# A third batch's u goes through the DMA transpose, the pair units' last product is cut in two, and the written order of all groups is drawn anew

## The chip, the core and the metric

The kernel runs on one core of a Trainium2 chip. Its engines are TensorE (PE, with its weight loads as PEld), VectorE (DVE), ScalarE (ACT), GpSimd (POOL) and SyncE (SP, which only issues transfers); each runs its own instructions in the order in which they were written. The metric is device time in microseconds (us). Times stand beside a profile, which is one execution recorded by the hardware.

## What is computed

Four batches of 768 steps with 8 heads of 48 columns (384 columns in all). First a gated linear recurrence, then a mixer that works along the steps with rank 32 and along the columns with a hidden width of 1536:

```python
for t in range(S):                                    # S = 768, per batch and head
    state = alpha[:, :, t, :, None] * state + einsum('bhd,bhe->bhde', k[:, :, t], v[:, :, t])
    y[:, :, t] = einsum('bhd,bhde->bhe', q[:, :, t], state)
x = y.transpose(0, 2, 1, 3).reshape(B, S, H * D)      # [4, 768, 384]
h = x.transpose(0, 2, 1) @ U @ V                      # U [768, 32], V [32, 768]
u = x + h.transpose(0, 2, 1)
out = u + relu(u @ w_ch1) @ w_ch2                     # w_ch1 [384, 1536], w_ch2 [1536, 384]
```

All inputs and the output are float32; the kernel multiplies in bfloat16.

## The kernel before

**Chunks.** Each batch b has six chunks c of 128 steps. Of a chunk, alpha, k, q and v are loaded as tiles of 128 steps x 8 heads x 48 columns, 192 KB each. All six chunks of batch 0 and the first four of batch 1 are worked as "pair units": two chunks are loaded together by halves of the heads, so that two neighbouring steps of a head lie in one run of 384 bytes (`pload`, line 350). The chunks of batches 2 and 3 and the last two of batch 1 are plain: one step of one head is a run of 192 bytes (`load`, line 357). The names below are those of the groups in the program, with b.c or b.half behind.

**A chunk's recurrence.** ACT takes the logarithm of alpha (lines 380 and 551), PE sums it along the steps, ACT takes exponentials, k and q are scaled by them (`rk`, lines 411 and 579, on POOL or DVE) and transposed on PE (`tr`, lines 428 and 592) or, for batch 3, by a DMA transpose that SP issues (`tkq`, line 604). Scores are masked (`pm`), multiplied with v (`rv`, cast by ACT or POOL), the state is carried on (`st`), and the result is copied out as x. In a pair unit the last product is `py`: 16 small matmuls (line 535) that need two masked tiles, one for the even heads and one for the odd.

**The mixer.** Per batch: the product with U (`xu`, line 702) and its copy (`utx`, line 713), the product with V chunk by chunk (`hb`, line 716), the sum u on DVE (line 717), and then u transposed, two chunks at a time. For the batches in `QUEUE_U` this is one DMA transpose on SP per two chunks (`tu`, line 722); for the others six PE transposes (`utr`, line 736) and a copy of the PSUM bank on ACT or DVE (`uev`, lines 277 and 279). `mlp1` (line 765) is 24 groups a batch, twelve for each half of the steps, of three matmuls each. The first half needs the transposes of chunks 0 to 3, the second those of chunks 2 to 5:

```python
if b in QUEUE_U:
    need = [(uT, "c", c) for c in ((0, 1), (1, 2))[tt]]
else:
    need = [(uT, 0), (uT, 1)] if tt == 0 else [(uT, 1), (uT, 2)]
```

A `relu` on ACT (line 775) or DVE (line 777) follows each; `mlp2` (line 791) is three groups of four matmuls for each chunk, then DVE adds u (line 797) and SP stores (lines 800 and 802).

**What sets the order.** Nothing is scheduled when the kernel is built. Every group is added to a plan, and the strings `TABLE` and `SLOTS` say in which order the groups are written, on which engine, and which buffer each takes. Three characters of `TABLE` are one group: two for its number and one for the engine (P for PE, A for ACT, D for DVE, G for POOL, S for SP; for a transfer the letter is the engine that issues it). "++" is a string of filler matmuls (line 270) that compute nothing. A group that needs another engine's result waits for it, and all that is written behind it on its own engine waits with it. Transfers are counted on eight semaphores in turn, so an engine that issues a transfer first waits for the one eight before it.

Of the kernel before, what the change touches and what calls it, by code (L numbers as in the profile page):

```python
# [16 lines left out]
ArA++BAASAvSA-AA3SQPAAySAsSCLA++BCNPAtSAzA++BA5ACOACPAAwS++BCiADSAECAAxSBAACRGAuS++BCSGCjACQACkPA4SClA++BCmAA7ADUPDVADWA  # L17
A0SC5ACTPCoGCUPCWABDSDXAEEPEGAA6SCpDA9ACVDCxPC7P++BCnACMAC9AAFGC+ABBSDrAA2SCyDCqPCsDCaPBHSCbDCXPCzPEFAA8SCrPCYDDtPCtAA1S
CcPCZDCeP++BCdDC8ADYGDaPCuPDZDCfPEIGDcAC-GDTGCwDEKPEHAAJPDbPC0DBCABFSABSDhPGCAAKADwA++BChACvDDiPDdDDjDEJGDvADuAA+SDePDgD
AGPELPAHADkPEMDC1PDfDBEAENABGSC2PBLSC3DDyGD0PD2ABISCgDBJSBKSBPSGEPDlDC6GGGADIPDJPDKDEOPDxGDLPDAGGHAEDGDBPC4DDzPDnPERPEPD  # L20
GFAAMSDMDALGDCPDDADmPDoPEQDESPD1AAQSDEABMSGJGDpAD3PGZAETDD5DDFPEUPDGDGIGDqAGbPDNPEVPGDGDOPD6P++BDsAGcADHDEWPEXAD4DD7PD8D
DPPDRAEYDGKPGMAD9PAYSGLPGNDACGADPD+PD-PEADGRPGSDDQAAEAEBAGOPGPDEZPEaPBTSGfGGwAGeAGdAEbAGyPG1ABNSGTD++BG0AEqPGQDBRSEoPGhP
GVPErDEkPGgGGWPGzABQAEcPEiPGjAEpDElDGiPGaGEsPHJAAUSAOGGXAEePEjDEtAAPGGkDGYAEdDHLPBOSHMAHNAEfDEmPGlPEnDANGGoPEgPGpDFGPGmD
GqDFHDFIPATABVSGnDFKPARGEhAFLAEwPExAASGFMPFNAE4PE2PAaGFQPE5DEyPBXSG2GBUSAZAFRDAbAFAPFJAE0PAcSE3ABSABZSFEPFFAGrDHOAG4PG6A
G3DHPDE1DFBAEuPHRPHTDFOPHQGEzDFPDG5PHiAFcPAXAFaPEvDG7AFdAAVAHSPHUDGsPGtPGuDBYSGvAG8PG+DAWGAhSBWSGxGGUGBaSAmSHVPBfSBrSG-P
FbAHkPHmAHoAFWPHADHBGE6PHXDH4AHnAFSPHlAG9DHqGFYPFTDH6PE7DH7AH8AHWDE+PHsPHuDHCDHpGE8PHKAFXAFZAHrPHtDFUPFVABbSE-AE9DHEPAgA
HFPHGPHYPHZDAfGBtSBjSHHDHvPHdPHIDHwDH+GIAPFCPAeGHaGAdAH9GHePFePHbDAiABcSHcDHxDICDFDAFkPF2PH-PIBDF8PIDPAlAHfPAjGAkGF9PBeS
HgAFwPBhSIFDHDGIEDHjABnSHyPH2PH3AH5AHzDH0DF3PFlPH1DIGPHhAApAFfPIHAIIPFxPIJAIQPISPAoGIKPAnGIRDITDAqGF+PFyPILDIMPINDFgPIYP
IZDF-DFzDF4PKCAKEPLBABkSIWPKFABzSJuAIXDIUPIOPIVAIPDKXAFmPFnDIaPBqSIbDJwPJxAF5DJ1DIiPKZPJvAIjAKdAI0PBlSFhDKGABdSAIGJyAJEP
JFABvSB1SIgPKKGJ2GI1AI+PI-AKIAIyPI4PKsAI5AIzAJGPIhDBiSI6PI7AJ0AJzAImPIqPKHAIrAInAKaAJKPIwPKDGJ+PJHAIkPKbAKuPKwAJIPLDPJLD  # L30
KcAKMPJ-DLWABwSJAPJJAIuPKyAJBAKfGIlDKeDKvAIxDBgSKJGLGAI2PI3DLHAIvAIcPLEABsSLIGIdAIePIfAKgPKiDJ3PBpSB0SIoPBmSJ5DLFAIpANFA
KxAIsPKhPItAJ4PKODKjAKSPKTDKLPJSPJTPJ6DBoSK0GJ7PLJGKNAB6SBySKUGKtGJ9DKkPKlDKPPKRDJUPLYPLZANHPKmDNJANKAKYGFqPFrPNNGKzGLKP
I8PNLAJ8DNIAKQDKnPBxSLaALcGKqPLMALLPLbDKoDKpGLNAB-SFsPK2PLdPK4DI9AKVPFtDK8PLfABuSK9DKrAJCPJDAK1PK3DLePNMGLgACDSK+GKAPKWA
JkPB3SB2SKBDB7SJVDB5SNWALOPNOSLPDK5PK6DLhPOMAJlPLQDK7DLCGLRPLSDLTGJmPNYPOOPCISORALXAN6ACESNbANoANcAJePLjDLUPLiDNaAK-PLAD
LVDJpPLkPJfPLlANZANPPNeGLmPLnAN8PN9ANGGN-ANQDJqPB4SLvPLtPN+ANRDOAANdGJrPCHSLwDOQALqPCCSLuDCASLxSLrDNXAOeALoPJYPLpDJMPNSP
# [821 lines left out]
```

## Time and profile before

| | |
|---|---|
| time, three runs | 158.62 us median (157.86 to 159.13) |
| span of the profiled execution | 156.8 us, 1.8 under the median |
| PE busy | 148.8 us, 95% of the span |
| DVE, ACT, POOL busy | 107.6, 90.0, 61.4 us |
| DMA | 31.53 MB, mean 201 GB/s |
| chain of waits | PE 84%, DMA 8%, DVE 4% |
| issued from ACT's queue (q10) | 2.16 MB of the 31.53 |

A page of the profile gives the busy time of each engine, then the span in 40 slices (tenths busy, the granted clock of PE, DMA share and GB/s), the chain that ended last, and groups of instructions by line. The granted clock of PE is 1.00 in every stretch shown. In a window row the pairs are busy time and, in brackets, the instructions of PE, PEld, DVE, ACT and POOL, and the last three numbers are the clock, the DMA share and GB/s. The DMA share counts the time that packets are in work on the 16 DMA engines, and can pass 1 where packets of two queues overlap.

### The profile page before, as it was taken

How to read it: one execution, taken by the hardware profiler on the slowest of the kernel's cores; microseconds unless marked ns; L12 is line 12 of the kernel's file. 1: busy time of each engine (PE TensorE's matmuls, PEld its weight loads, DVE VectorE, ACT ScalarE, POOL GpSimd, SP SyncE). 2: the span in 40 equal slices, each digit the busy share in tenths (PEclk: the TensorE clock that was granted, in tenths of full speed). 3: DMA queues.
4: the chain of work that ended last, by engine and by line, in shares of the span. 5: the costliest groups of instructions: out<-in, count | busy, mean ns of one | idle time of the engine just before them, and what ended most of it. 6: DMA issues, size and time to landing. Idle time of an engine off the chain costs nothing.

```text
span 156.8 us, 4413 instructions
## 1 busy us (share of the span) xinstructions
PE 148.8 (95%) x1715; PEld 97.7 (62%) x1715; DVE 107.6 (69%) x236; ACT 90.0 (57%) x234; POOL 61.4 (39%) x95
## 2 busy tenths in 40 slices
PE   2878999999999999999999999999999999999992
PEld 0456678666767656666668666665667555556662
DVE  6038899987899628816588976885989580673162
ACT  3678889986978272999958585379232202450000
POOL 8285995756088600136679261052623000000000
PEclk9999999999999999999999999999999999999999
DMA  5999999999988989989989996897976346345625
GB/s 145 319 323 326 268 301 313 344 265 268 280 239 193 270 161 191 189 169 211 208 169 214 134 222 119 169 181 145 176 144 151 105 87 139 127 129 151 199 100 201
DMA packets 98291, 31.53 MB, mean 201 GB/s; under 512 B 91968, under 2 KB 98240, under 8 KB 98272
## 3 DMA queue, kind: packets, MB, share of 16 engines
q1 hardware_dynamic: 92464, 29.11, 80.6%
q10 hardware_dynamic: 5808, 2.16, 5.2%
q8 instruction: 13, 0.21, 0.6%
q14 instruction: 6, 0.05, 0.1%
HBM read 23.79 MB, written 4.72 MB: 182 GB/s over the span
## 4 chain that ended last, share of the span: by engine, by line
PE 84%; DMA 8%; DVE 4%; ACT 1%; issue 1%; ACTq 0%; DVEq 0%
PE ps L791 30%; PE ps L765 29%; DMA io<-in_alpha_dram 8%; PE ps L716 3%; PE ps L620 3%; PE ps L592 2%; PE ps L687 2%; PE ps L428 2%; PE ps L535 2%; PE ps L558 2%; PE ps L682 1%; PE ps L736 1%; PE ps L452 1%; PE ps L643 1%; PE ps L702 1%; DVE rkq L411 1%
## 5 line engine op out<-in xcount | busy, mean ns | idle before, releaser
L791 PE MATMUL ps<-w_sb,h1t 128*128 128x384 bf16 (+2 forms) x300 | 53.1, 319 | 0.0
L765 PE MATMUL ps<-uT,w_sb 128*128 128x384 bf16 x288 | 51.0, 326 | 0.1
L775 ACT ACTIVATE h1t<-ps 128x384 bf16<-128x384 f32 x58 | 27.2, 509 | 19.1 <-PE ps L765 19.0
L791 PEld LDWEIGHTS <-h1t 128*128 128x128 bf16 x300 | 27.3, 97 | 15.9 <-issue 0.6
L765 PEld LDWEIGHTS <-w_sb 128*128 128x128 bf16 x288 | 27.0, 98 | 16.3 <-issue 0.4
L777 DVE TENSOR_SCALAR h1t<-ps 128x384 bf16<-128x384 f32 x38 | 20.1, 552 | 19.4 <-PE ps L765 15.9
L579 POOL TENSOR_TENSOR rkq<-io,aa 128x384 bf16<-128x384 f32 x12 | 11.7, 975 | 23.0 <-ACT aa L569 13.2
L630 DVE TENSOR_TENSOR pm<-ps,maskc 128x512 bf16<-128x512 f32 x28 | 17.7, 681 | 2.8 <-PE ps L620 2.8
L717 DVE TENSOR_TENSOR ub<-xb,ps 128x384 bf16<-128x384 bf16 x24 | 12.2, 549 | 6.9 <-PE ps L716 6.9
L797 DVE TENSOR_TENSOR io<-ub,ps 128x384 f32<-128x384 bf16 (+2 forms) x25 | 12.9, 531 | 3.7 <-PE ps L791 3.6
L277 ACT CAST xb<-ps 128x192 bf16<-128x192 f32 (+1 forms) x21 | 8.2, 393 | 10.6 <-PE ps L687 7.9
L463 DVE TENSOR_TENSOR pm<-ps,maskp 128x512 bf16<-128x512 f32 x20 | 13.2, 682 | 0.5 <-PE ps L452 0.2
L277 ACT COPY kqt<-ps 128x512 bf16<-128x512 bf16 x18 | 10.5, 608 | 1.6 <-PE ps L428 0.8
L579 POOL TENSOR_TENSOR rkq<-io,ai 128x384 bf16<-128x384 f32 x9 | 8.2, 914 | 6.9 <-PE ps L643 3.9
L411 POOL TENSOR_TENSOR rkq<-io,ai 128x384 bf16<-128x384 f32 x9 | 8.5, 945 | 6.1 <-ACT lt L380 3.1
L568 ACT ACTIVATE ai<-ps 128x384 bf16<-128x384 f32 x14 | 7.0, 502 | 5.6 <-PE ps L560 3.1
L654 POOL TENSOR_TENSOR st<-sm,tot 128x384 bf16<-128x384 f32 x8 | 6.9, 868 | 8.2 <-DVE sm L670 8.0
L571 ACT ACTIVATE tot<-ps,off 128x4 f32<-128x4 f32 x22 | 5.6, 279 | 5.3 <-PE ps L560 3.4
L279 DVE COPY kqt<-ps 128x512 bf16<-128x512 bf16 x18 | 7.3, 417 | 1.4 <-PE ps L592 0.9
L428 PE MATMUL ps<-ident,rkq 128*128 128x128 bf16 x80 | 8.0, 228 | 0.1
L281 POOL CAST w_sb<-h1t 128x384 bf16<-128x384 f32 x14 | 6.8, 516 | 2.9 <-DMA h1t<-in_moe_w_ch_dram 2.9
L411 POOL TENSOR_TENSOR rkq<-io,aa 128x384 bf16<-128x384 f32 x7 | 6.4, 910 | 3.4 <-ACT aa L404 2.3
(111 smaller groups left out, 224.5 us busy)
## 6 DMA issues: line engine op xcount, KB each, us to landing
io<-in_v_dram SPq DMA_DIRECT2D x22, 192.0 KB, 4.1
io<-in_q_dram SPq DMA_DIRECT2D x22, 192.0 KB, 4.4
io<-in_k_dram SPq DMA_DIRECT2D x21, 192.0 KB, 4.0
io<-in_alpha_dram SPq DMA_DIRECT2D x20, 192.0 KB, 4.3
out_dram<-io SPq DMA_DIRECT2D x13, 192.0 KB, 2.0
h1t<-in_moe_w_ch_dram SPq DMA_DIRECT2D x4, 576.0 KB, 6.0
h1t<-in_moe_w_ch_dram SPq DMA_DIRECT2D x3, 768.0 KB, 6.6
out_dram<-io SPq DMA_DIRECT2D x20, 96.0 KB, 2.2
```

Source lines behind the costliest of these rows:

```text
L277: nc.scalar.copy(dst, src)
L411: eng.tensor_tensor(jh(dst()[:, :, 0:D]), raw(a), jh(x()), op=ALU.mult)
L428: nc.tensor.matmul(dst, lhsT=ring()[:, HP * j + 2 * a : HP * j + 2 * a + 2, :].rearrange("t h w -> t (h w)"), rhs=ident, start=True, stop= ...
L463: nc.vector.tensor_tensor(dst, s2, maskp.to_broadcast([C, 2, 2, C]), op=ALU.mult)
L579: eng.tensor_tensor(dst()[:, :, 0:D], a(), x(), op=ALU.mult)
L630: nc.vector.tensor_tensor(pm()[:, :, par, :], s2, maskc.to_broadcast([C, HP, C]), op=ALU.mult)
L717: P.add(f"u {b}.{c}", lambda e, c=c, hb=hb: nc.vector.tensor_tensor(ub()[:, c, :], xb()[:, c, :], hb()[:, 0:DM], op=ALU.add), r=[hb] + xk( ...
L765: nc.tensor.matmul(hb()[:, 0:TW], lhsT=w1_sb[:, ct, jt * 128 : (jt + 1) * 128], rhs=u_half(uT, ct, tt, b in QUEUE_U), start=(ct == 0), sto ...
L775: nc.scalar.activation(dst, hb()[:, 0:TW], AF.Relu)
L777: nc.vector.tensor_scalar_max(dst, hb()[:, 0:TW], 0.0)
L791: nc.tensor.matmul(hb()[:, 0 : hi - lo], lhsT=h1()[:, jt, c * C : (c + 1) * C], rhs=w2_sb[:, jt, lo:hi], start=(jt == 0), stop=(jt == NJ - 1),
L797: P.add(f"out_{hi - lo} {b}.{c}", lambda e, hb=hb, lo=lo, hi=hi: nc.vector.tensor_tensor(flat(ou)[:, lo:hi], ub()[:, c, lo:hi], hb()[:, 0 ...
```

## The change

Five things change in the text.

1. `QUEUE_U` takes batch 1 in. Its 18 PE transposes and three copies go; three DMA transposes of 128 x 768 values, issued by SP, come. Line 722 of before is line 741 of the changed kernel.
2. `py` becomes two groups of eight matmuls, the even heads and the odd, each of which needs only its own masked tile. The matmuls are the same 160.
3. The pool of `utx` has three buffers instead of two.
4. A branch for batches in `INPLACE` is added, and that tuple is empty, so none of its code is built.
5. `TABLE` and `SLOTS` are new. Besides the order this changes engines. Of the `rv` casts ACT has 8 instead of 12 and POOL 16 instead of 12; of the weight casts ACT 5 (10) and POOL 19 (14); of the relus ACT 62 (58) and DVE 34 (38); of the plain and pair `st` groups five go from POOL to DVE, and two `utx` copies from ACT to DVE. ACT issued 11 pair loads before, all at the start; now it issues one of them and 18 of the plain loads in the middle. There are 3 filler matmuls instead of 11.

```diff
@@
-ArA++BAASAvSA-AA3SQPAAySAsSCLA++BCNPAtSAzA++BA5ACOACPAAwS++BCiADSAECAAxSBAACRGAuS++BCSGCjACQACkPA4SClA++BCmAA7ADUPDVADWA
...
+AASAFGArACLA++CCNPAvSCjAClPA3SDVADXAPJAPtSAsSAxSCPACSGCUPAGPCQACOAAuSCnAAwSCqDCsPCRDCTPDaAAKDCWDCMGCaPCmACpDCrPAzSCVDAyS
...
-    QUEUE_U = (2, 3)
+    QUEUE_U = (1, 2, 3)
+    INPLACE = ()
@@
-    utxs = Pool(slots("utx", 2, [128, DM], BF16))
+    utxs = Pool(slots("utx", 3, [128, DM], BF16))
@@
-        def f_y(e):
-            for h in range(HP):
+        def f_y(e, par):
+            for h in range(par, HP, 2):
                 for j in range(2):
                     for c in range(2):
                         r = slice(64 * c, 64 * c + 64)
                         nc.tensor.matmul(
-                            yb[c]()[:, h * D : (h + 1) * D], lhsT=pm()[r, (h // 2) * 2 + j, h % 2, :], rhs=rv()[r, HP * j + h, :],
+                            yb[c]()[:, h * D : (h + 1) * D], lhsT=pm()[r, (h // 2) * 2 + j, par, :], rhs=rv()[r, HP * j + h, :],
                             start=(h == 0 and j == 0 and before[c] is None), stop=(h == HP - 1 and j == 1), skip_group_check=True,
                         )
...
-        P.add(f"py {b}.{u}", f_y, r=[rv, (pm, 0), (pm, 1)], w=[yb[0], yb[1]])
+        for par in range(2):
+            P.add(f"py {b}.{u}", lambda e, par=par: f_y(e, par), r=[rv, (pm, par)], w=[yb[0], yb[1]])
@@
         utx = Buf(utxs)
         P.add(f"utx {b}", lambda e: copy(e, utx(), xu()[:, 0:DM]), r=[xu], w=[utx])
+        if b in INPLACE:
...
-            if b in QUEUE_U:
+            if b in INPLACE:
+                need = [(uT, "t", tt, j) for j in range(NCT)]
+            elif b in QUEUE_U:
                 need = [(uT, "c", c) for c in ((0, 1), (1, 2))[tt]]
```

Three places of the order follow. In these rows io is a landing buffer of a load, uT a transposed u, ub the u before it, kqt a transposed k or q, h1t the hidden tile (and, for the weights, a landing buffer), lt a logarithm and rv the cast v.

SP in the middle of batch 2's loads, before:

```order
54 L357 DMA io_150<-in_alpha_dram 128x8x48
55 L357 DMA io_152<-in_k_dram 128x8x48
56 L357 DMA io_154<-in_alpha_dram 128x8x48
57 L357 DMA io_157<-in_v_dram 128x8x48
58 L357 DMA io_159<-in_q_dram 128x8x48
```

The same stretch of SP now:

```order
58 L358 DMA io_150<-in_alpha_dram 128x8x48
59 L741 DMA_TRANSPOSE uT_212<-ub_206 128x6x128
60 L358 DMA io_152<-in_q_dram 128x8x48
61 L741 DMA_TRANSPOSE uT_212<-ub_206 128x6x128
62 L358 DMA io_155<-in_alpha_dram 128x8x48
63 L358 DMA io_157<-in_k_dram 128x8x48
64 L741 DMA_TRANSPOSE uT_212<-ub_206 128x6x128
65 L358 DMA io_159<-in_q_dram 128x8x48
```

The three transposes of batch 1's u stand among the loads of batch 2, each with a load or two ahead of it and behind it.

SP at the transposes of batch 2's u, before:

```order
83 L357 DMA io_148<-in_k_dram 128x8x48
84 L357 DMA io_142<-in_alpha_dram 128x8x48
85 L357 DMA io_145<-in_v_dram 128x8x48
86 L357 DMA io_149<-in_k_dram 128x8x48
87 L722 DMA_TRANSPOSE uT_212<-ub_207 128x6x128 x2
88 L357 DMA io_155<-in_k_dram 128x8x48
89 L357 DMA io_150<-in_q_dram 128x8x48
90 L357 DMA io_159<-in_q_dram 128x8x48
91 L722 DMA_TRANSPOSE uT_212<-ub_207 128x6x128
```

The same place now:

```order
84 L823 DMA out_dram<-io_158 64x384
85 L358 DMA io_154<-in_v_dram 128x8x48
86 L358 DMA io_157<-in_k_dram 128x8x48
87 L606 DMA_TRANSPOSE kqt_189<-rkq_81 128x8x128
88 L606 DMA_TRANSPOSE kqt_192<-rkq_80 128x8x128
89 L741 DMA_TRANSPOSE uT_213<-ub_207 128x6x128 x3
90 L358 DMA io_166<-in_q_dram 128x8x48
```

All three transposes of batch 2's u now follow each other, and two transposes of batch 3's k and q stand right ahead of them, where loads stood.

ACT in the first half of batch 1's `mlp1`, before:

```order
126 L775 ACTIVATE h1t_73<-ps 128x384 x3
127 L571 ACTIVATE tot_187<-ps,off 128x4
128 L551 ACTIVATE lt_77<-io_150 128x8x48
129 L775 ACTIVATE h1t_73<-ps 128x384 x3
130 L571 ACTIVATE tot_185<-ps,off 128x4 x2
131 L571 ACTIVATE tot_187<-ps,off 128x4
132 L775 ACTIVATE h1t_73<-ps 128x384 x2
133 L568 ACTIVATE ai_184<-ps 128x384
```

ACT in the same stretch now:

```order
119 L358 DMA io_162<-in_q_dram 128x8x48
120 L796 ACTIVATE h1t_73<-ps 128x384 x3
121 L278 COPY kqt_192<-ps 128x512
122 L358 DMA io_166<-in_alpha_dram 128x8x48
123 L796 ACTIVATE h1t_73<-ps 128x384 x2
124 L358 DMA io_167<-in_v_dram 128x8x48
125 L553 ACTIVATE lt_76<-io_153 128x8x48
126 L553 ACTIVATE lt_75<-io_155 128x8x48
127 L278 COPY kqt_192<-ps 128x512
128 L796 ACTIVATE h1t_73<-ps 128x384 x3
```

Loads that SP issued now stand on ACT, between relus (line 775 before, line 796 now).

At the start of ACT's program the instruction that loads its function table (line 825 before, 848 now) stood ahead of the first logarithm. It now stands behind ten activations, and the built program has three such loads: one ahead of the first logarithm, one between the third logarithm and the first exponential, and one at line 848.

More of the change, by code (lines that the diff above doesn't have):

```diff
@@ L21 @@
[L21 to L35, printed above, removed]
@@ new lines @@
+MgPMhDMjDMnAJjSORPOSAMkPF1SOcSOdPNnPMlAOtPMzPNHPNoDMuPMvPOuDOeDOfDOvDM0POjPOwPOxANpDNtPNuAOkDNIPNJPOyPOzAM1PM9PO0PO1DO2P
+O3DO4SO7PO8DO5PO6DMwPM+PM-PO+PO-DPAPNCPNDPPBDNEPM4PM5PM6PO9SPLPPCSPFPNADPMDMxDPbPPXPPGANKDPDPPEAPYAPlPPNPPRPPmDPODM2DJdS
+NFDM7DPHPJXSM3SPIAPjPPJPPKAPkDPdPPpPPhPPZPPqAPSDPcAPvPPTPPfPPUAPaANLSPVPJpSPgAP9PNBSPPPPtPJvSJeSPeAJYSP4PFpSNGSFvSPwAFuS
+PiAQMPPxPPzPPWDQRPM8SPQDP+PP-PJkSGASJ0SPyAPnPPoDP5PQADQBSMySPrPPsAQSPP0PFoSQNPPuAQOPP1PP2DQPDP6PP7DQTPQUDQQSP3SQCPQVSP8S
+QDPQEPQFDQGSQHPQIPQJPQKDQLS
@@ L779, in mlp1, with mlp2 @@
             P.add(f"relu {b}.{tt}.{jt}", g, r=[hb], w=[(h1, tt, jt)], after=casts[jt] if b == 1 else ())
-    def mlp2(b, ub, h1, c):
+    def mlp2(b, ub, h1, c, xb, utx):
         tt = c // NT
@@ L786, in mlp2 @@
             hb = Buf(bank)
+            if b in INPLACE:
+                P.add(f"hbo {b}.{c}", lambda e, hb=hb, lo=lo, hi=hi: nc.tensor.matmul(hb()[:, 0 : hi - lo], lhsT=(ve_sb if paired(b, c) else vm_sb)[:, c * C : (c + 1) * C], rhs=utx()[:, lo:hi], start=True, stop=False), r=[utx, ("ve" if paired(b, c) else "vm", c // NT)], w=[hb])
             for g in range(3):
@@ L819 @@
                 whole = [(x, 0, x)]
-        stage_mix(b, xb, ub, uT)
+        utx = stage_mix(b, xb, ub, uT)
         mlp1(b, uT, h1, 0)
@@ L823 @@
         for c in range(NC):
-            mlp2(b, ub, h1, c)
+            mlp2(b, ub, h1, c, xb, utx)
     P.add("table", lambda e: nc.scalar.preload_act_table_set("natural_log_exp_and_others"))
```

63 lines of the change are left out of this document (44 added, 19 removed).

## The prediction

> **What bounds the kernel now.** I read the page first, for the engines and the slices:
>
> ```profile
> span 156.8 us, 4413 instructions
> PE 148.8 (95%) x1715; PEld 97.7 (62%) x1715; DVE 107.6 (69%) x236; ACT 90.0 (57%) x234; POOL 61.4 (39%) x95
> PE   2878999999999999999999999999999999999992
> DMA  5999999999988989989989996897976346345625
> ```
>
> PE is the busy engine, but the DMA row also reads 8 or 9 up to the 23rd slice. So I took the table of windows, to see where each of the two binds:
>
> ```profile
> 5.00:25.00 20.00, 18.15 (x331) 12.60 (x331) 13.09 (x29) 16.61 (x45) 14.68 (x19) 1.00 1.15 303
> ...
> 50.00:65.00 15.00, 15.00 (x164) 9.71 (x162) 10.38 (x22) 7.40 (x18) 3.34 (x7) 1.00 0.98 209
> 65.00:80.00 15.00, 15.00 (x141) 9.81 (x139) 7.53 (x16) 13.39 (x40) 8.54 (x11) 1.00 0.98 193
> 80.00:95.00 15.00, 15.00 (x216) 10.51 (x213) 13.19 (x25) 11.30 (x31) 9.40 (x12) 1.00 1.02 187
> 95.00:120.00 25.00, 25.00 (x229) 15.86 (x228) 20.37 (x39) 11.79 (x30) 7.14 (x8) 1.00 0.88 158
> ```
>
> From 50 to 120 us PE never stops, and its clock is 1.00. The DMA engines are about full there too (0.98 to 1.02 up to 95 us). The two are in balance: PE sets the time, with DMA close behind. The chain of waits gives the milestones:
>
> ```profile
> 32.86 3.91 PE ps L765 x24
> ...
> 101.13 0.97 PE ps L765 x6
> ...
> 146.97 7.02 PE ps L791 x52
> 154.02 0.30 DVE io L797
> ```
>
> The first `mlp1` starts at 32.86, batch 2's first at 101.13, PE ends at 153.99, and 2.8 us of sum and store close the span. The three runs' median of 158.62 lies 1.8 above this execution's 156.8; I add 1.8 to every span below.
>
> **The PE ledger.** What leaves PE is batch 1's transposes, and what moves is read by group:
>
> ```profile
> 62.06 0.67 PE ps L736 x12
> ...
> 63.38 0.33 PE ps L736 x6
> 63.95 0.51 PE ps L765 x3
> ...
> 40.34 0.22 PE ps L428 x4
> ...
> 31.80 0.35 PE ps L452 x16
> ```
>
> The 18 transposes are 0.67 + 0.33 = 1.0 us, in a stretch where PE has no gap, so they count in full. The new order puts four `tr` groups (0.22 each) and two score groups of pair units (0.35 each) ahead of the first `mlp1` that stood behind it: 1.6 us leaves the saturated part for a part in which, up to 25 us, PE was busy 18.15 of 20. I take the first `mlp1` at 32.9 as before: the gaps of 1.85 us and eight filler matmuls fewer make room for 1.6. With nothing waiting, PE ends at 153.99 − 1.0 − 1.6 = 151.4, the span is 154.2 and the time 156.0.
>
> `py` in two: the same 160 matmuls. The trace shows such groups at two lengths,
>
> ```profile
> 52.56 0.20 PE ps L535 x16
> ...
> 15.83 0.30 PE ps L535 x16
> L535 PE MATMUL ps<-rv,pm 64*128 64x48 bf16 x160 | 3.7, 181 | 0.1
> ```
>
> so ten more group starts cost at most 10 × 0.10 = 1.0 us, if each second half stands apart, and gain at most the 0.1 us that this line waited. Most lie before 50 us; I take 0 and keep 1.0 for the range. The third `utx` buffer can only remove waits, and none for it is in the chain: 0, both ways. Batch 1's three copies of the transposed u leave ACT and DVE, where they lie beside PE work, which has no gap at 62 to 64 us: 0.
>
> **The added DMA transposes.** Each costs what batch 2's and 3's do:
>
> ```profile
> L722 SPq DMA_TRANSPOSE uT<-ub x6: 1217/1242/1366, 95.6 to 129.4; - x6
> DMA to landing us min/median/max: 2.8/2.8/3.3
> ```
>
> SP spends 1.24 us on one, and it lands 2.8 us after its issue. For batch 1, before, the last PE transpose began at 63.38 and `mlp1` at 63.95, 0.6 us later; a DMA transpose needs 2.8, 2.2 more. That is covered by batch 0's `mlp2` (0.65 us a group, of which the new order has six between the last product with V and the first `mlp1`), so 0; 2.2 us if the cover goes. The dearer side is what is queued behind them. In the order they stand among batch 2's loads on SP, so these loads go out 3 × 1.24 = 3.7 us later.
>
> **The DMA ledger.** Here the sum turns. Plain and paired loads have different rates. In the window from 57 to 85 us only plain loads run, in that from 5 to 25 mostly paired ones:
>
> ```profile
> GB/s 227 192 199 238 147 199 176 194 208 189 179 195 229 99 120 213 140 238 168 218 212 183 204 237 197 223 201 220 212 195 200 235 89 159 160 162 259 211 195 158
> DMA packets 28167, 5.38 MB, mean 192 GB/s; under 512 B 28163, under 2 KB 28163, under 8 KB 28163
> ...
> GB/s 323 324 324 323 322 324 324 324 321 323 323 326 322 325 322 324 321 325 326 321 348 302 310 313 305 323 278 166 182 253 297 254 312 345 302 309 312 319 277 139
> q10 hardware_dynamic: 3704, 1.38, 25.1%
> ```
>
> A plain load of 196.6 KB at 192 GB/s takes 1.02 us of all DMA engines, at the best slices (237 to 238) 0.83, and a paired one at 323 takes 0.61. In the second row the rate is flat although ACT's queue has a share in some slices only. So I take a second queue as no faster. In the Trainium skill, "Trainium Kernel Development and Optimization", section "Key Constraints", transfers issued from SP, ACT and POOL run on the same 16 DMA engines, and issuing from several only saves issue time; the flat 321 to 326 agrees, and by it the 18 loads on ACT give no bandwidth.
>
> Now what must land before batch 2's `mlp1` can start, which is its first two transposes of u. Before:
>
> ```profile
> 92.11 1.18 SPq L357 DMA_DIRECT2D io<-in_k_dram  x1
> 95.59 2.55 SPq L722 DMA_TRANSPOSE uT<-ub  x2
> ...
> SPq L722 <- DVE ub L717: 6.4, 2, 3.2
> SPq L604 <- POOL rv L281: 2.0, 1, 2.0
> ...
> L604 SPq DMA_TRANSPOSE kqt<-rkq x6: 1237/1256/2283, 85.9 to 114.4; - x6
> out_dram<-io SPq DMA_DIRECT2D x20, 96.0 KB, 2.2
> ```
>
> The second of them was issued at 95.59 + 1.3 and landed at 99.7, 1.4 us before it was needed; SP had waited 3.2 us for u just before. Counted over the order, now ahead of it stand four more plain loads (4.1 us), batch 1's three transposes (3.7), one more `tkq` (1.25) and three more half stores (96 KB at 192 GB/s, 1.5): 10.5 us more. Without the 3.2 us of waiting it lands at 99.7 − 3.2 + 10.5 = 107.0. PE needs it at 101.13 − 2.6, and 0.6 later for other groups that the order moves in front: at 99.1. It is 7.9 us late. Part comes back, because a queue that runs late no longer waits: 2.0 us before a `tkq` (the row above), and the slices of the 57 to 85 window at 99, 120, 140 and 89 GB/s, where loads waited for buffers, are worth 1.2 us in 28, so 1.6 over the 37 us from 50. That leaves a stall of 7.9 − 3.6 = 4.3 us. Bounds: the DMA share of 0.98 against 1.15 in the first window is 15% of 45 us, 6.6 us reclaimed at most, a stall of 1.3; nothing reclaimed, 7.9.
>
> **Loads issued from ACT.** An engine that issues a transfer first waits for the one eight before it, and everything behind waits too. Rows of before:
>
> ```profile
> ACT rv L277 <- DMA io<-in_alpha_dram: 1.5, 1, 1.5
> 8.45 0.37 ACTq L350
> L775 ACT ACTIVATE h1t<-ps 128x384 bf16<-128x384 f32 x58 | 27.2, 509 | 19.1 <-PE ps L765 19.0
> ```
>
> An ACT cast stood 1.5 us behind such an issue. Eight of the 18 loads now stand among the relus of batch 1's `mlp1`, where ACT was busy 13.39 of 15 us. Issuing alone, about 0.4 us each by the row of 0.37, is 3.2 us against an idle 1.6 us. The excess of 1.6 us is what PE can lose by it, less what other PE groups cover: I take 1.0. Bounds: 0 if every slot is free, and one wait of 1.5 us at four of the eight, 6 us in all, if not. The casts and relus that change engine leave ACT's and POOL's sums within about 3 us of before: 0.
>
> **Table loads.** There are three instead of one:
>
> ```profile
> 0.00:10.00 10.00, 6.62 (x41) 3.52 (x42) 2.56 (x23) 5.04 (x11) 5.40 (x19) 1.00 0.91 252
> ...
> L825 ACT ACT_TABLE_LOAD x1 | 1.3, 1283 | 1.8 <-issue 1.8
> ```
>
> Two more are 2.6 us of ACT, in the first 10 us, where ACT was busy 5.04 of 10 and the chain waits for alpha loads. I take 0; 2.6 if they land in the chain. The Trainium skill, "ScalarE: Activation LUTs", section "What ACT_TABLE_LOAD costs", gives 1283 ns, which the row repeats, and about 1380 ns of drain for every switch, which no run here shows; by it two would be 5.3 us. Either delay comes ahead of a DMA-bound stretch, so it would not add to the stall in full.
>
> **Sum.** 154.2 + 4.3 + 1.0 = 159.5; plus 1.8 is 161.3.
>
> **The rivals.**
> Faster, 156.0: the loads keep up and PE's 2.6 us stand. That needs plain loads at no more than about 0.85 us: 37 of them by 0.17 is 6.3, with the 2.0 wait above the 7.9 us. For it speak slices at 235 to 259 GB/s and DMA gaps behind SP's waits; against it a mean of 192 with DMA engines full. Chance 0.22.
>
> Same, about 158.5: most of the 6.6 is reclaimed (stall 1.3) and ACT adds 1, or the start loses the 2.6 us while the loads keep up. Chance 0.20.
>
> Slower by much, 165: ACT is held as long as its loads are, relus of batch 1 free their PSUM banks late and PE stops at 66 to 80 us as well: four waits of 1.5 us instead of 1.0 gives 161.3 + 5 = 166.3, and as the loads go on while PE stops, I take a third off the later stall of 4.3. For it: eight loads among those relus. Against it: the one wait of this kind that the trace shows is 1.5 us, with 11 loads on ACT. Chance 0.14.
>
> That the change doesn't do what it says isn't open: the order shows the transposes gone from PE.
>
> **How the numbers follow.** My forecast has the remaining 0.44, 161.3. Within 1%, which is 157.0 to 160.2 and about what a measurement can tell from no change, lies the same case, 0.20; faster 0.22; slower 0.44 + 0.14 = 0.58. The forecast's own range is from 158.3 (stall 1.3) to 164.9 (nothing reclaimed). The range for 8 in 10 takes in the faster case at 156.0 and reaches to 165.0, which leaves out half of the slowest case and the far side of the fast one.
>
> **What would show it.** If I am right, the trace has PE idle for 3 to 5 us, put down to an SP DMA transpose of u, at the first `mlp1` of batch 2 near 99 to 104 us; SP without its 3.2 us wait; the DMA share at 1.0 or more from 50 to 100 us with a rate still near 200 GB/s; ACT waiting for DMA in front of load issues. If instead PE stays full there and the rate climbs to 235 GB/s, the DMA ledger is wrong and the faster rival holds. If PE stops between 66 and 80 us waiting for relus, ACT's issues decide. A first `mlp1` past 34 us would point to the table loads or to the fewer fillers.

## The result: 174.0 us, 9.7% slower

The changed kernel takes 174.0 us in the median (173.1 to 175.0, four runs) against 158.4 for the kernel before on the same chip. The ratio is 1.097, with a 95% interval from 1.090 to 1.104. The profiled execution has a span of 171.8 us, 15.0 more than the 156.8 of before. Here and below a median takes in all runs and a ratio only undisturbed ones, so the two can differ a little.

The page, the table of windows and the chain of waits of the changed kernel, in the rows that answer to those shown of before (a window row has the stretch, then busy us and instructions of PE, PEld, DVE, ACT and POOL, then clock, DMA share and GB/s):

```profile
span 171.8 us, 4374 instructions
PE   2699999999998199999539999989997999999992
DMA  5999999999999996999999791699950027077136
...
50.00:65.00 15.00, 10.55 (x83) 5.98 (x82) 6.41 (x14) 7.08 (x20) 5.98 (x12) 0.89 1.12 250
65.00:80.00 15.00, 15.00 (x131) 9.66 (x130) 9.90 (x19) 8.50 (x22) 6.73 (x10) 1.00 1.02 178
80.00:95.00 15.00, 10.09 (x112) 6.60 (x110) 7.83 (x17) 7.40 (x22) 3.42 (x4) 1.00 1.37 223
95.00:120.00 25.00, 24.39 (x257) 15.72 (x255) 19.98 (x38) 12.82 (x37) 10.98 (x14) 1.00 0.84 138
...
36.89 3.41 PE ps L786 x21
...
168.82 0.30 DVE io L820
```

Before, PE was full in each of the four windows. Now it stands 4.45 us in the first, 4.91 in the third and 0.61 in the last. The first `mlp1` (line 786) starts at 36.89 instead of 32.86, 4.0 us later. From 120 us to its end at 168.8 PE stands another 1 us (a window row not shown here). That is 15.0 us of stops and late start, and 12.4 once the 2.6 us of PE work that left or moved ahead are taken off. PE ends 14.8 us later than before. Of the 2.4 us between, the clock, which is shown below, gives 1.7 (5 us at 0.66); 0.7 us is not placed. The timeline of PE has the stops with the idle time before each in brackets, and that of ACT what happened meanwhile:

```profile
59.49 0.81 PE L814 MATMUL ps<-w_sb,h1t 128*128 128x384 bf16 x4 [3.71 <-ACT h1t L796]
...
84.70 0.65 PE L786 MATMUL ps<-uT,w_sb 128*128 128x384 bf16 x3 [1.72 <-ACT h1t L796]
87.55 0.65 PE L786 MATMUL ps<-uT,w_sb 128*128 128x384 bf16 x3 [1.73 <-ACT tot L573]
90.35 0.38 PE L594 MATMUL ps<-ident,rkq 128*128 128x128 bf16 x4 [1.46 <-ACT aa L571]
...
53.02 4.09 ACTq L358 DMA_DIRECT2D io<-in_k_dram  x1
57.13 1.77 ACTq L358 DMA_DIRECT2D io<-in_v_dram  x1
58.95 0.49 ACT L796 ACTIVATE h1t<-ps 128x384 bf16<-128x384 f32 x1 [5.28 <-issue]
```

PE's four long stops all wait for ACT, and at the first of them ACT was issuing two loads, which took 4.09 and 1.77 us instead of the usual 0.4. The relu behind them stood 5.28 us. The profile puts this wait down to issue: it shows no earlier transfer that these two loads waited for. Their issuing itself was long, and SP's issue of a load at 53.77 us took 2.57 us as well. The three stops at 84 to 90 us differ. The activations that PE waits for there stand 3.31, 2.17 and 1.93 us, and the last two of these waits are put down to older loads that had not landed. SP was held as well, and right behind PE's first stop the granted clock is down:

```profile
56.59 0.75 SPq L358 DMA_DIRECT2D io<-in_alpha_dram  x1
65.31 1.30 SPq L741 DMA_TRANSPOSE uT<-ub  x1
...
SPq L741 <- DVE kqt L280: 9.0, 1, 9.0
...
59.50:64.50 5.00, 5.00 (x24) 2.27 (x24) 1.35 (x3) 3.94 (x11) 2.15 (x4) 0.66 1.02 176
```

From 57.3 to 65.3 SP issued nothing (8.0 us by the timeline; the row of waits has 9.0), because the first transpose of batch 1's u stood at its head and u was late. The row names a copy by DVE; what the transpose reads is u, and DVE wrote its sums from 63.6 to 65.7 us (line 736). All loads of batch 2 behind it on SP waited too.

The stop that I had forecast, batch 2's transposes at the first `mlp1` of that batch, is the last and smallest entry of one row:

```profile
L786 PE MATMUL ps<-uT,w_sb 128*128 128x384 bf16 x288 | 52.5, 326 | 4.1 <-ACT tot L573 1.7 <-ACT h1t L796 1.7 <-DMA uT<-ub 0.6
```

### The profile page after: what moved, and what is told of

The parts are those of the page before. It is cut to its first block, busy times and chain, and to the rows that moved or that the text cites. A ratio compares the mean times of both kernels' runs of the same rounds, so it can differ in the third digit from the quotient of the medians.

```text
span 171.8 us, 4374 instructions
## 1 busy us (share of the span) xinstructions
PE 152.7 (89%) x1690; PEld 99.3 (58%) x1690; DVE 107.6 (63%) x236; ACT 90.1 (52%) x229; POOL 60.6 (35%) x99
## 4 chain that ended last, share of the span: by engine, by line
PE 57%; DMA 14%; SPq 7%; issue 6%; DVE 5%; POOL 3%; ACT 3%; ACTq 2%; POOLq 1%; DVEq 0%
PE ps L814 24%; PE ps L786 13%; DMA io<-in_alpha_dram 6%; SPq L358 5%; DMA h1t<-in_moe_w_ch_dram 4%; PE ps L429 3%; DMA kqt<-rkq 3%; DMA io<-in_v_dram 2%; ACTq L358 2%; POOL rkq L581 2%; PE ps L735 2%; PE ps L453 2%; PE ps L487 2%; DVE ub L736 1%; PE ps L622 1%
## 5 line engine op out<-in xcount | busy, mean ns | idle before, releaser
L786 PE MATMUL ps<-uT,w_sb 128*128 128x384 bf16 x288 | 52.5, 326 | 4.1 <-ACT tot L573 1.7
L796 ACT ACTIVATE h1t<-ps 128x384 bf16<-128x384 f32 x62 | 28.3, 500 | 40.2 <-PE ps L786 31.5
L814 PEld LDWEIGHTS <-h1t 128*128 128x128 bf16 x300 | 28.1, 99 | 22.0 <-issue 6.6
L798 DVE TENSOR_SCALAR h1t<-ps 128x384 bf16<-128x384 f32 x34 | 18.2, 551 | 14.0 <-PE ps L786 13.8
L581 POOL TENSOR_TENSOR rkq<-io,ai 128x384 bf16<-128x384 f32 x12 | 11.2, 944 | 17.8 <-ACT ai L570 10.6
L736 DVE TENSOR_TENSOR ub<-xb,ps 128x384 bf16<-128x384 bf16 x24 | 12.1, 549 | 7.4 <-PE ps L735 7.3
L464 DVE TENSOR_TENSOR pm<-ps,maskp 128x512 bf16<-128x512 f32 x20 | 13.1, 684 | 0.6 <-PE ps L453 0.4
L581 POOL TENSOR_TENSOR rkq<-io,aa 128x384 bf16<-128x384 f32 x9 | 8.4, 948 | 11.6 <-ACT aa L571 8.4
L282 POOL CAST w_sb<-h1t 128x384 bf16<-128x384 f32 x19 | 9.0, 507 | 9.7 <-DMA h1t<-in_moe_w_ch_dram 9.7
L282 POOL CAST rv<-io 128x384 bf16<-128x384 f32 x16 | 8.3, 525 | 7.4 <-DMA io<-in_v_dram 7.4
L412 POOL TENSOR_TENSOR rkq<-io,aa 128x384 bf16<-128x384 f32 x9 | 8.2, 912 | 6.5 <-ACT aa L405 3.9
L429 PE MATMUL ps<-ident,rkq 128*128 128x128 bf16 x80 | 8.8, 256 | 1.5 <-POOL rkq L412 1.5
L571 ACT ACTIVATE aa<-ps 128x384 bf16<-128x384 f32 x14 | 7.1, 518 | 4.3 <-PE ps L562 4.1
L412 POOL TENSOR_TENSOR rkq<-io,ai 128x384 bf16<-128x384 f32 x8 | 7.3, 924 | 4.4 <-ACT ai L404 1.9
```

Source lines behind the costliest of these rows:

```text
L282: nc.gpsimd.tensor_copy(dst, src)
L412: eng.tensor_tensor(jh(dst()[:, :, 0:D]), raw(a), jh(x()), op=ALU.mult)
L429: nc.tensor.matmul(dst, lhsT=ring()[:, HP * j + 2 * a : HP * j + 2 * a + 2, :].rearrange("t h w -> t (h w)"), rhs=ident, start=True, stop= ...
L464: nc.vector.tensor_tensor(dst, s2, maskp.to_broadcast([C, 2, 2, C]), op=ALU.mult)
L581: eng.tensor_tensor(dst()[:, :, 0:D], a(), x(), op=ALU.mult)
L736: P.add(f"u {b}.{c}", lambda e, c=c, hb=hb: nc.vector.tensor_tensor(ub()[:, c, :], xb()[:, c, :], hb()[:, 0:DM], op=ALU.add), r=[hb] + xk( ...
```

## The experiments

Four theories stood against each other. A: ACT is held by the loads that it issues. B: the DMA engines are short, whoever issues, which was the forecast. C: at the start one issuing queue moves less than two. D: DMA transposes that wait for u hold SP's loads behind them. All times are compared with runs of the kernel before on the same chip.

**The plain loads back to SP.** In the changed kernel's table the letter of 18 loads goes from A to S; one of them:

```diff
-BeA        (load 2.0, issued by ACT)
+BeS        (load 2.0, issued by SP)
```

> The changed kernel with its 18 plain loads of ACT issued by SP instead, at the same places of the written order. Theory A (ACT's queue is held by the loads it issues; in the changed kernel PE lost 3.71 us at 59.5 behind a relu that stood 5.28 us behind load issues, and 1.72 + 1.73 + 1.46 us at 84 to 90 behind activations that stood behind load issues): these stops go, 6 to 9 us come back, about 165 to 168 us. Theory B (the DMA engines are short, as forecast): the same loads need the same engines, the stops stay and are put down to DMA, 172 to 175 us; or SP, which now issues all, holds its own loads behind its waits for u and it gets slower.

169.8 us, ratio 1.065 (1.058 to 1.072): 4.2 us come back (5.1 by the ratios, which set each kernel against the kernel before on its own chip), less than theory A had, but a clear change for the same loads on the same DMA engines. The stop at 59.5 and the three at 84 to 90 are gone (PE stands 1.8 us from 50 to 65 and 0.6 from 80 to 95). A new one of 2.77 us has come at 97.7:

```profile
91.60 4.23 DMA io<-in_q_dram
...
96.83 0.84 POOL st L656
...
97.72 0.33 PE ps L684 x4
```

This one is a late load of q, by way of POOL's scaled q and the state. Behind it the granted clock is down too, though the stop is shorter than 3 us:

```profile
98.00:102.00 4.00, 4.00 (x40) 1.86 (x36) 1.02 (x2) 2.38 (x8) 1.62 (x4) 0.58 0.98 201
```

So of the 8.6 us of ACT's four stops about half comes back, and the other half turns up again as loads that land late and as the clock behind them.

**The same 18 loads on ACT, in the kernel before.** The reverse edit: 18 letters from S to A in the old table, nothing else.

```diff
-BeS        (load 2.0)
+BeA        (load 2.0)
```

> The kernel before with the same 18 plain loads issued by ACT as in the changed kernel, at the places where SP issued them in the written order. Theory A (ACT is held by the loads that it issues): PE stops behind relus and exponentials between 50 and 95 us, 3 to 10 us in all, 162 to 169. Theory B (DMA only): the same loads, no change, 158 to 160.5.

168.1 us, ratio 1.063 (1.057 to 1.068): 9.7 us more. The timelines of PE and ACT and the windows show how:

```profile
69.54 0.65 PE L765 MATMUL ps<-uT,w_sb 128*128 128x384 bf16 x3 [2.08 <-ACT h1t L775]
...
89.45 1.13 ACTq L357 DMA_DIRECT2D io<-in_v_dram  x1
95.65 0.38 ACTq L357 DMA_DIRECT2D io<-in_q_dram  x1
96.07 0.94 ACT L551 ACTIVATE lt<-io 128x384 bf16<-128x384 f32 x2 [7.11 <-DMA io<-in_k_dram]
...
96.64 0.48 PE L558 MATMUL ps<-lt,ut_ones 128*128 128x384 bf16 x1 [5.49 <-ACT lt L551]
...
80.00:90.00 10.00, 10.00 (x151) 7.21 (x150) 8.29 (x17) 6.61 (x16) 9.12 (x12) 1.00 0.37 74
96.60:103.00 6.40, 6.36 (x66) 4.16 (x65) 1.02 (x2) 3.42 (x10) 1.36 (x2) 0.58 0.52 87
```

The issue of q on ACT waited until 95.65 for an older load, and a logarithm behind it stood 7.11 us, PE 5.49 us behind that. It works the other way as well: from 80 to 90 us the DMA engines were busy only 37% of the time at 74 GB/s (before, 172 GB/s in the same 10 us at a share of 0.98), because loads on ACT came late behind ACT's own work. Theory A holds in the old order too, and theory B, which had no change here, falls as the whole account.

**Batch 1's transposes alone.** The kernel before with three DMA transposes, each behind the second of its two u, in place of three PE groups and three copies:

```diff
-    QUEUE_U = (2, 3)
+    QUEUE_U = (1, 2, 3)
-IUP ... IOP ... IVA ... IPD ... IaP ... IbD   (utr 1.3, utr 1.1, uev 1.3, uev 1.1, utr 1.5, uev 1.5)
+tu 1.3, tu 1.1, tu 1.5 on SP, each behind its u
```

> The kernel before with batch 1's u transposed by three DMA transposes alone, each issued by SP at the place behind the second of its two u, everything else as it stood. What the forecast has of it: PE 1.0 us less work; 2.2 us of landing that nothing covers in the old order, as mlp1 followed the last PE transpose by 0.6 us; loads of batch 2 held 3.7 us on SP and 3.7 us more DMA work, of which SP's waits further on (3.2 and 2.0 us) take up all or nearly all. Sum: +1 to +3 us, 159.5 to 162. If DMA transposes are what broke the changed kernel, it is 165 or more; if the loads behind them have slack, 158 to 160.

165.3 us, ratio 1.044 (1.039 to 1.048): 7 us, more than twice what the forecast's sum had at most. PE's timeline, its windows, and SP's transposes:

```profile
63.49 1.58 SPq L722 DMA_TRANSPOSE uT<-ub  x1
...
68.33 2.10 PE L765 MATMUL ps<-uT,w_sb 128*128 128x384 bf16 x6 [3.69 <-DMA uT<-ub]
...
62.00:68.00 6.00, 2.06 (x18) 1.04 (x16) 3.03 (x7) 3.47 (x9) 0.91 (x1) 0.87 1.03 153
68.00:74.00 6.00, 5.67 (x20) 2.81 (x21) 0.56 (x1) 2.04 (x6) 0.91 (x1) 0.56 1.21 214
DMA to landing us min/median/max: 2.8/3.1/4.8
```

The last transpose took 4.8 us to land among the loads of batch 2, not the 2.8 to 3.3 of the transposes before, which were issued after 95 us when fewer loads ran. PE stood 3.69 us for it, and then ran 6 us at a granted clock of 0.56.

**The gap filled.** The same kernel with 16 filler matmuls in front of the waiting group:

```diff
+++Q        (16 fillers, ahead of mlp1 1.1.0)
```

> The kernel before with batch 1's u by DMA transposes alone, and 16 filler matmuls (0.22 us each, 3.5 us) put in front of the mlp1 group at which PE stood 3.8 us. In that run the granted clock was 0.56 from 68 to 74 us, right behind the stop. If the clock falls because PE stood idle, it stays at 1.00 and about 2 us of the 7.0 come back, 162.5 to 164, though the wait itself stays. If the clock has another cause, nothing comes back, 165 to 166.5.

164.0 us, ratio 1.033 (1.026 to 1.039). PE's timeline and the same windows:

```profile
65.95 3.61 PE L270 MATMUL ps<-h1t 128*128 128x512 bf16 x16
69.75 2.45 PE L765 MATMUL ps<-uT,w_sb 128*128 128x384 bf16 x14 [0.19 <-DMA uT<-ub]
...
68.00:74.00 6.00, 5.81 (x35) 3.06 (x33) 0.56 (x1) 2.86 (x8) 0.91 (x1) 1.00 1.10 197
```

The wait is the same, and the clock stays at 1.00: 35 matmuls are recorded in the window where 20 were. So the idle time itself lowers the clock. In the timelines it takes 17.0 us from the start of batch 1's `mlp1` to its first `mlp2`, against 19.5 without fillers and 13.2 in the kernel before. Of these 2.5 us the medians show 1.4 (1.7 by the ratios, whose intervals just touch). The profiled execution with fillers also had a granted clock of 0.83 from 5 to 25 us, so its span can't be set against the other.

**The transposes with the order mended.** The three transposes, `py` in two, and batch 1's first-half `mlp1` groups ahead of the second-half ones, so that the last transpose is needed 12 groups later:

```diff
-mlp1 1.0.3, 1.1.0, 1.1.8, 1.0.2, 1.1.5, 1.0.11, ...
+mlp1 1.0.3, 1.0.2, 1.0.11, 1.0.5, 1.0.7, 1.0.10, ...   (then 1.1.0, 1.1.8, ...)
```

> The kernel before with batch 1's u by DMA transposes, the pair units' last product in two groups, and batch 1's mlp1 groups put in another order: all twelve of the first half, which need the first two transposes, ahead of the twelve of the second, which need the last (in the run with the transposes alone PE stood 3.8 us at 64.2 for the last one, at a group of the second half that stood third). If the wait is only a matter of order, it goes, or leaves 1 us, and the 1.0 us of PE transposes is gained: 157 to 159. If the loads held behind the transposes on SP are late as well, PE stops later in batch 2 instead: 160 to 164.

159.8 us, ratio 1.011 (1.008 to 1.014). The wait is gone; what is left is 0.60 and 0.33 us of idle PE in the first two windows (before, none), so even then the 1.0 us of PE work was not gained. The time is still 1.5 us above the kernel before, and the rest of that is not placed:

```profile
50.00:65.00 15.00, 14.40 (x146) 8.75 (x145) 10.11 (x21) 7.14 (x19) 3.07 (x7) 1.00 0.96 202
65.00:80.00 15.00, 14.67 (x137) 9.33 (x135) 6.76 (x14) 13.04 (x38) 7.04 (x9) 1.00 1.14 194
80.00:95.00 15.00, 15.00 (x215) 10.51 (x213) 13.24 (x25) 11.05 (x29) 9.20 (x13) 1.00 1.02 189
```

Batch 2's loads had the slack to bear the three transposes. The price in the run with the transposes alone was the stop and the clock, not DMA work.

**Batch 1's u on PE in the changed kernel.** Its plain loads on SP, and its three DMA transposes replaced by PE groups and copies again (`QUEUE_U = (2, 3)`, three groups placed ahead of the first `mlp1` groups that need them):

```diff
-    QUEUE_U = (1, 2, 3)
+    QUEUE_U = (2, 3)
```

> The changed kernel with its plain loads on SP and batch 1's u transposed by PE again (three groups of six, ahead of batch 1's mlp1, with their copies on ACT and DVE). Theory D (the transposes that wait for u hold SP's loads behind them: 9.0 us in the changed kernel, about 4 us in the run with the loads on SP): these waits go, batch 2's loads come 3 to 5 us earlier, PE pays 1.0 us, and the time falls from 169.8 to 165 to 168. Theory B (DMA engines short): three transposes less are 3.7 us of DMA work less, which comes out about the same; only the place tells, a wait of SP or a full DMA row. If neither matters, 170 to 171.

164.1 us, ratio 1.037 (1.030 to 1.045): 5.7 us less than with the loads on SP alone (4.4 by the ratios). Its windows and the first `mlp1`:

```profile
80.00:95.00 15.00, 15.00 (x185) 10.32 (x180) 12.66 (x24) 10.82 (x29) 5.18 (x6) 1.00 0.99 198
95.00:120.00 25.00, 25.00 (x247) 15.74 (x245) 20.23 (x40) 12.93 (x37) 10.90 (x14) 1.00 1.01 180
...
38.96 3.09 PE ps L786 x19
```

PE is full again from 80 to 120 us. That is what theory D expected, at about its size. It doesn't separate SP's hold from the 3.7 us of DMA work, as the expectation said; for the hold speaks the changed kernel's DMA row from 64 to 72 us, in slices of 0.2 us:

```profile
DMA  8578996200000999960257999999695633689999
```

The engines ran dry for about 1 us behind the held transpose, in a stretch where 5.38 MB of plain loads in 28 us had kept them full before. That is less than the gain, so how the gain divides between SP's hold and the DMA work stays open.

**Pair loads.** In the changed kernel SP issues all pair loads but one. Two runs turned on that: in the kernel before, the ten pair loads of ACT after its first go to SP; and in the changed kernel with its plain loads on SP, the same eleven pair loads as before go to ACT.

```diff
-A-A, AzA, ...     (pair loads 0.5, 0.2, ... on ACT, kernel before)
+A-S, AzS, ...     (on SP)
```

> The kernel before with the ten pair loads that ACT issued after its first given to SP, at their places in the written order, as the changed kernel has it. Theory C (one queue moves less: the changed kernel moved 278 GB/s from 5 to 30 us from SP's queue alone, the kernel before 315 from two): the rate falls to about 280, 0.9 MB or 3 us are missing by 30 us, the first mlp1 is 1 to 3 us later than 32.7, the time is 160 to 163. Theory B (the DMA engines set the rate, whoever issues, as the forecast had it): 315 GB/s, 158 to 159.

> The changed kernel with its plain loads on SP, as in the run before of that kind, and besides with the same eleven pair loads issued by ACT as in the kernel before. Theory C (at the start SP's issue time is the limit: the changed kernel issues nearly all pair loads on SP at about 0.55 us each in an unbroken row up to 30 us, and moved 244 to 294 GB/s from 8 to 27 us, where the kernel before moved 265 to 344): the rate goes back to 300 GB/s or more, every later load is earlier by 2 to 3 us, the first mlp1 moves from 35.2 to 33 to 34, and the time falls by 2 to 5 us from 169.8, to 165 to 168. Theory B (DMA engines are the limit, whoever issues): same rate, 169 to 170.5.

The first gave 159.5 us, ratio 1.006 (1.001 to 1.010). Its window from 5 to 30 us, and that of the kernel before under it:

```profile
5.00:30.00 25.00, 23.04 (x454) 16.13 (x452) 17.80 (x40) 21.32 (x60) 17.02 (x22) 1.00 1.06 286
```

```profile
5.00:30.00 25.00, 23.15 (x454) 16.22 (x453) 17.97 (x41) 21.35 (x60) 17.29 (x23) 1.00 1.13 315
```

One queue moved 286 GB/s, two 315: theory C is right about the rate, and the 0.7 MB that is missing costs 0.9 us by the ratio, less than the 2.5 us that it takes to move at 286 GB/s. A DMA share above 1 needs no second queue: SP's queue alone has 106.1% from 10 to 25 us in this run. The Trainium skill, "DMA: Bandwidth & Descriptors", section "Issuing engines are not separate DMA queues", says that a second issuing engine only saves issue time, usually small against the transfer. The forecast leaned on a like sentence; here the difference was 9% in rate, and the runs don't show whether issue time or the engines' overlap made it.

The second gave 186.1 us, ratio 1.163 (1.153 to 1.173), 16 us slower than without. The same loads on ACT, at the places that the new order gives them, were far worse than on SP: PE's longest stop there was behind a scaled k or q,

```profile
46.57 1.03 PE L429 MATMUL ps<-ident,rkq 128*128 128x128 bf16 x8 [6.83 <-POOL rkq L412]
...
POOL rkq L412 <- DMA io<-in_k_dram: 11.7, 3, 7.5
POOL rkq L412 <- DMA io<-in_q_dram: 11.3, 2, 7.8
```

and that waited for k and q, whose issues stood behind ACT's activations. It is no test of theory C, as ACT's place in the order changed with it; it is theory A's other side, as at 80 to 90 us above.

**`py` in two, alone.** The old table with each `py` followed by its second half.

```diff
-        P.add(f"py {b}.{u}", f_y, r=[rv, (pm, 0), (pm, 1)], w=[yb[0], yb[1]])
+        for par in range(2):
+            P.add(f"py {b}.{u}", lambda e, par=par: f_y(e, par), r=[rv, (pm, par)], w=[yb[0], yb[1]])
```

> The kernel before with the pair units' last product in two groups that follow each other directly, everything else as it stood. The forecast took 0, with up to 1.0 us more if each half pays its start again and at most 0.1 us of gain: 158 to 160.

158.2 us, ratio 0.998 (0.995 to 1.001): nothing, as forecast.

**The start.** Three runs on the changed kernel: the table load moved ahead of the first logarithm, so that one is built instead of three; eleven fillers at the old positions instead of three; both, with the plain loads on SP.

```diff
 ArA        (pload 0.0)
+QWA        (table, moved up from the 43rd place of the list)
 CLA        (ln 0.0)
```

> The changed kernel with the table load put ahead of the first logarithm, so that one such load of 1.28 us is built instead of three. If the start is lost to the table loads, the first mlp1 moves from 36.9 us towards 34.3 and the time falls by up to 2.6 us, to 171.4. If they were hidden beside the first alpha loads, or what follows waits for DMA anyway, no change: 173 to 174.5.

> The changed kernel with eleven filler matmuls at the same positions of the written list as before, instead of three. If PE is slow at the start because it is not kept at work (its 128x384 matmul of line 390 took 0.43 to 0.44 us up to 17.5 us, where in the kernel before line 389 took 0.32 from 11.4 us on), the fast rate comes earlier and the first mlp1 moves by 1.5 to 3 us towards 34; the time falls by the same at most, 171 to 172.5. If not, the fillers add 8 x 0.2 to 0.4 us, 174 to 176.

> The changed kernel with all three edits: loads on SP, table load first, eleven fillers. If the start (4.0 us late) and ACT's held queue (about 8.6 us) are the two causes and add up, 160 to 163 us. If the DMA engines set the time, 170 or more, as the start's gain is given back at the first wait for a load.

173.9 us, ratio 1.092 (1.086 to 1.098); 175.4, 1.094 (1.086 to 1.102); and 169.0, 1.062 (1.055 to 1.068). In the timelines of these profiles the first `mlp1` came at 35.6, 34.8 and 36.0 us, against 36.7 in the changed kernel's, and neither edit alone moved the time beyond its interval. The stops behind ACT are in both traces (3.60 and 3.52 us at the first of them). That they took a gain back is not shown: with the loads on SP and nothing else changed, the first `mlp1` came at 35.2 us, about as early. With the loads on SP the two together gave 0.8 us, within the intervals.

**What was left.** Since 5.7 us remained after the loads and the transposes, the start was mended once more where nothing later should take it back: the last version (loads on SP, u on PE) with the table load first and eleven fillers.

```diff
+QWA        (table, ahead of ln 0.0)
+++B        (one filler, eleven times)
```

> The changed kernel with its plain loads on SP, batch 1's u on PE, the table load ahead of the first logarithm, and eleven fillers at the positions of before. The run with the first two alone was 164.1 us, 5.7 above the kernel before; its first mlp1 began at 38.8 us against 32.7, and its PE lost 15.6 us ahead of it against 11.0 (matmuls at 0.57 instead of 0.35 us a group of 16 up to 25 us). If the start is what is left, the first mlp1 comes at 35 to 36 and the time falls by 2 to 4 us, to 160 to 162. If loads that come late later on take it back, as they did where table load and fillers were changed alone (173.9 and 175.4 against 174.0), it stays at 163 to 165.

165.4 us, ratio 1.039 (1.033 to 1.045): nothing gained. So neither table loads nor fillers are the remaining 5.7 us. The first `mlp1` came at 37.7 us in the profiled execution, not at 35 to 36, but the granted clock there was 0.50 from 26.5 to 33.3 us, so its start says little.

One thing at the start differs from execution to execution. Up to 50 us the changed kernel, the run with the loads on SP and the run with u on PE have the same order on every engine. Yet in their timelines the first `mlp1` came at 36.7, 35.2 and 38.8 us. The score groups of the pair units (16 matmuls, line 452 before and 453 now) show a difference. The rows are of the kernel before, the loads on SP, the changed kernel and u on PE:

```profile
15.41 0.42 PE L452 MATMUL ps<-kqt 48*64 48x128 bf16 x16
...
14.61 0.42 PE L453 MATMUL ps<-kqt 48*64 48x128 bf16 x16
...
18.90 0.64 PE L453 MATMUL ps<-kqt 48*64 48x128 bf16 x16
...
24.41 0.64 PE L453 MATMUL ps<-kqt 48*64 48x128 bf16 x16
```

The kernel before has 0.42 us from the first such group, at 13.1 us, on. The other three have 0.64 us for the last time at 12.1, 18.9 and 24.4 us, in the order of their first `mlp1`. The clock column reads 1.00 in these stretches and doesn't show it. No run changed this alone, so that it delays the first `mlp1` is likely, and not shown.

## Why the prediction was wrong, point by point

**The sign** was right and the size was not: 161.3 with a range to 165.0, against 174.0. The sign was right by luck. It came from a stall of 4.3 us that turned out 0.6; without that stall the forecast's own sum is 154.2 + 1.0 + 1.8 = 157.0, faster than before. Of the four causes that the runs point to, the forecast had two as terms that were too small (ACT's loads, the transposes), one at nothing (the start) and one not at all (the clock).

**"Loads issued from ACT: I take 1.0."** This is the step that failed first. I priced the issue time against ACT's idle time, and the rival that ACT is held by its loads at four waits of 1.5 us, with a chance of 0.14. Measured: 4.2 us in the changed kernel (5.1 by the ratios) and 9.7 us in the old order for the same 18 loads. The row that I had (one wait of 1.5 us) came from the start, where loads ran at 0.61 us each; between 50 and 95 us a load takes 1.0 us, and the loads that ACT's issues waited for landed 5 to 6 us after their own issue (4.9 and 5.6 us in the chains of waits of the old order and of the changed kernel). I did not scale the wait to the fuller queue; that it grows with the queue is a reading, as no run varied it alone. The longest stop of the changed kernel, 3.71 us at 59.5, had no term at all: there the issues themselves took 4.09 and 1.77 us, which I had priced at 0.4. Why they took so long stays open. The forecast looked for such stops at 66 to 80 us, where PE was full; they came at 56 to 59 and 83 to 90. I also counted only one direction. An engine that computes also makes its loads late, as the 37% busy DMA engines at 80 to 90 us show.

**"The added DMA transposes … 0; 2.2 us if the cover goes", and loads "3.7 us later".** The transposes' landing of 2.8 us was read where few loads ran; among batch 2's loads it was up to 4.8 (and 5.5 in the changed kernel). The wait on SP was priced as issue time, 3 x 1.24. It is rather the whole time that u is late, 9.0 us once u itself stood behind PE's stop. In the chain of waits SP then issues loads without a break from 74.4 to 83.2 us, and the load issued at 83.3 holds ACT, and PE behind it, up to 90.4. So a stop of PE became a stop of loads and that a second stop. Three transposes cost 5.7 us (4.4 by the ratios) in the changed kernel with its loads on SP, and 7.0 in the old order, where 1.5 us is left once the order suits them (159.8 with `py` in two, against 158.3).

**"The DMA ledger … a stall of 4.3 us" at the first `mlp1` of batch 2.** It was 0.6 us there. The arithmetic added DMA work as if PE would arrive on time; by then PE had already stopped for 9 us, and from 95 to 120 us the DMA engines were no longer full (0.84 at 138 GB/s). That loads are close to their limit was right, and shows where ACT's stops are taken away: half of ACT's stops is lost to the late load at 97.7. But with u on PE, and so three transposes fewer, the same DMA engines, full at 0.99 to 1.01, fed PE without a stop from 80 to 120 us. DMA capacity was not the bound that the forecast made of it.

**What had no term: the clock.** Stops of 3.71 us (changed kernel), 3.69 us (transposes alone) and 5.49 us (loads on ACT in the old order) were followed by 5 to 6 us at 0.56 to 0.66. The trace of before has no such stop and so could not show it. The Trainium skill, "TensorE: Matmul & The Clock Gate", section "HAM oscillation — how this bites in real kernels", says that PE gaps over about 3.4 us bring the throttle back. The stops of 3.69, 3.71 and 5.49 us agree; behind the 2.08 us stop at 69.5 the clock row of that run shows no drop. But the stop of 2.77 us in the run with the loads on SP is shorter than that, and 0.58 came behind it. With the table load first, two stops of 1.58 and 1.72 us at 84.4 and 87.3 were followed by 0.50 from 87.2 to 90.4 us, and in the changed kernel nearly the same two were not. So these runs give no length below which a stop is free.

**"I take the first `mlp1` at 32.9."** It came at 36.9 in the chain, and at 35.4 with the loads on SP, where PE's groups reached their shorter length earlier. So some 2.5 us do not hang on that. Work of 1.6 us moved ahead did not find room in the start's gaps. The table loads (0 taken, 2.6 as bound) moved the first `mlp1` by 1.2 us at most and the time by nothing, so the sign named in the forecast, a first `mlp1` past 34 us, pointed to neither of its two causes.

**What held:** `py` in two is worth nothing; in the changed kernel the faster rival's condition (loads keep up) was not met. The 1.0 us of removed PE work is in the rows of before, but no run gained it. And "a second queue as no faster" was wrong in rate (286 against 315 GB/s) but worth only 0.9 us.

**What stays open:** with loads on SP and u on PE the new order is still 5.7 us slower. In that profile its first `mlp1` is 6.1 us later than before, of which 1.6 is work moved ahead, and PE stands 2.8 us behind it; together that is 7.3 of the 7.5 us by which the span is longer. So most of it lies ahead of the first `mlp1`. But this profiled execution took 166.2 us, 2.1 more than the other three, and its matmuls of the start were the longer ones up to 24.4 us. Which part of the new order of the start makes the rest is not shown; table loads and fillers don't. The casts, relus and state updates that changed engine, and the third `utx` buffer, were not run alone.

## What to carry to other kernels

Issue loads from an engine whose queue holds nothing that PE waits for. Price a load on a computing engine by the time until the transfer eight before it lands, in both directions, and not by the shortest issue seen: under load one issue took 4.09 us. A transfer that waits for a result belongs behind the loads on its queue, not among them, and its landing is to be read from a stretch as loaded as its new place. Where PE may stand for some 3 us, count the slow clock behind the stop with it.

## What was not expected of the hardware

The granted clock fell to 0.56 behind a 3.69 us stop of PE and to 0.58 behind one of 2.77 us. It stayed at 1.00 when 16 useless matmuls filled the wait of 3.69 us, and that kernel's median was 1.4 us lower. Issuing one load took ACT 4.09 us where 0.4 is usual, with no wait that the profile shows. Two issuing queues moved 315 GB/s of the same transfers where one moved 286. And a DMA transpose landed after 2.8 us or after 4.8, by the loads around it.
